# Keys of two attention pairs in one buffer, parted by VectorE: a grouped-query attention kernel on one Trainium2 core

## The chip, the core and the metric

The kernel runs on one NeuronCore of a Trainium2 chip. The core has a matrix engine (TensorE, "PE" in the profile, its weight loads "PEld"), three engines for elementwise work (VectorE "DVE", ScalarE "ACT", GpSimd "POOL"), a queue engine that issues transfers here (SyncE, "SP"), and 16 DMA engines that move data between the chip's memory and the on-chip buffers. The metric is the device time of one execution in microseconds. A profiled execution also has a span, which is the time between its first and its last recorded event.

## What is computed

The reference, cut to what matters:

```
B, Hq, Hkv, Sq, Sk, D = 16, 32, 8, 16, 2048, 128      # all tensors bf16
k = repeat(k, 4, axis=1);  v = repeat(v, 4, axis=1)   # 4 query heads share one key/value head
scores = einsum("bhqd,bhkd->bhqk", q, k) * D ** -0.5
out = einsum("bhqk,bhkd->bhqd", softmax(scores), v)
```

There are 16 * 8 = 128 groups (one key/value head of one batch entry). Each has 4 * 16 = 64 query rows, 512 KB of keys and 512 KB of values. K and V together are 128 MB, read once; queries and output are 2 MB each.

## The kernel before

**Tiling.** Two groups make a pair, so there are NP = 64 pairs, numbered p. Each pair has 1 MB of K, 1 MB of V and 128 rows of queries. Everything is a software pipeline over p, with one loop written out by hand for each engine and semaphores between them. The first four pairs and the last ones are unrolled, the middle runs in a hardware loop of 8 (4 on TensorE).

**One pair, engine by engine.**

- SyncE's queue loads K of a pair into one of 8 buffers `Kn` and V into one of 4 buffers `Vb`. The helper `load` (L178, built on `copy`, L171) describes a 1 MB load as 64 rows of 16 KB on the memory side and 128 partitions of 8 KB on the buffer side, so each row of 16 KB is spread over two neighbouring partitions. Only the first two loads of K are plain (128 rows of 8 KB).
- VectorE's `kt(p)` (L474 to L483, the instruction is L482) turns the keys of a pair: it sees each key's 128 bf16 numbers as 64 f32 words and transposes 32x32 blocks of 2048 words in each partition into one of two buffers `KT`.
- TensorE's `scores(p)` (L353) multiplies the queries `Qs` with `KT` into `S_ps`, the only score buffer in PSUM: it waits for `kt(p)` and for VectorE to have read the scores of the pair before (`sem_max`).
- VectorE's `step(p)` (L490) waits for these scores, reads `S_ps` in two halves, writes them scaled to `Sneg` and takes the row minimum (L502, called max(p) below); then, at odd p, it computes two reciprocals (L488); then it runs `kt(p + 2)`. VectorE runs its instructions in this order and no other.
- GpSimd joins the minima of the two halves (L225 to L233), and ScalarE computes the exponentials (`exp`, L550).
- TensorE transposes the exponentials (`transposes`, L371), ScalarE copies them to `PT` (`evict`, L561), and four pairs later (PVLAG = 4) TensorE multiplies them with V (`product`, L423, or L412 for the last 8 pairs). ScalarE scales the result (`norm`, L574) and stores it: one store of 32 KB a pair for pairs 0 to 39 and for the last one; the outputs of the others are held in `Oh` and stored in six pieces at the end.

**The order of the loads.** SyncE's queue runs one loop over t: K of pair t, then now and then a block of queries, then V of pair t - VLAG with VLAG = 6. A load of K waits until the buffer that it overwrites has been turned (`sem_kt`), a load of V until the product that used its buffer is done (`sem_pv`). The last four V loads go into freed `Kn` buffers and wait for nothing that is late. All these loads are on one queue and land in the order in which they are issued.

**The end.** For the last four pairs TensorE's order is written out by hand (L454 to L470): scores(62), six filler matmuls (`idle`, L433), product(57), scores(63), transposes(61), product(58), product(59), transposes(62), product(60), transposes(63), product(61), five fillers, product(62), three fillers, product(63). ScalarE's order is exp(61), norm(57), exp(62), evict(61), norm(58), exp(63), evict(62), norm(59), evict(63), and then the last norms and the last store. V of pair 63 is loaded in two pieces of 768 KB and 256 KB (L307).

Of the kernel before, what the change touches and what calls it, by code (L numbers as in the profile page):

```python
# [6 lines left out]
ALU = mybir.AluOpType  # L7
# [5 lines left out]
NV = 4  # L13
NKT = 2
NPT = 4
NO = 8
NQ = 2
NR = 8
VLAG = 6
PVLAG = 4  # L20
QLEAD = 3
HELD = (4, 4, 4, 4, 4, 3)
# [3 lines left out]
def bass_standalone__gqa_softmax__sampling_kernel(  # L26
# [3 lines left out]
    v: bass.AP,  # L30
    out: bass.AP,
):

# [19 lines left out]
    sb = lambda name, shape, dt: ctx.enter_context(nc.sbuf_tensor(name, shape, dt))  # L55
    sem = lambda name: ctx.enter_context(nc.semaphore(name))

    iota_t = sb("iota_t", [128, 128], I32)
    ident4 = sb("ident4", [128, 128], F32)
    warm = sb("warm", [128, 2], F32)  # L60
    Kn = [sb(f"Kn{i}", [128, 32 * 128], BF16) for i in range(NK)]
    Vb = [sb(f"Vb{i}", [128, 32 * 128], BF16) for i in range(NV)]
    KT = [sb(f"KT{i}", [128, 32 * 64], F32) for i in range(NKT)]
    Qn = [sb(f"Qn{i}", [128, 4, 128], BF16) for i in range(NQ)]
    Q4 = sb("Q4", [128, 4, 2, 4, 64], BF16)
    QT = [sb(f"QT{i}", [128, 2, 512], F32) for i in range(2)]
# [15 lines left out]
    O_ps = ctx.enter_context(nc.psum_tensor("O_ps", [128, 512], F32))  # L82

    sem_id = sem("sem_id")
    sem_k = [sem(f"sem_k{i}") for i in range(NK)]
    sem_v = [sem(f"sem_v{i}") for i in range(NV)]
    sem_vl = [sem(f"sem_vl{i}") for i in range(2)]
    sem_vx = [sem(f"sem_vx{i}") for i in range(3)]
# [20 lines left out]

    qf = q.rearrange("b h s d -> (b h s) d")  # L110
    of = out.rearrange("b h s d -> (b h s) d")
    kf = k.rearrange("b h s d -> (b h s d)").rearrange("(r x) -> r x", x=4096)
    vf = v.rearrange("b h s d -> (b h s d)").rearrange("(r x) -> r x", x=4096)
    vf4 = v.rearrange("b h s d -> (b h) (s d)").rearrange("g (a x) -> a g x", a=128)

# [15 lines left out]


    def v_tile(p):
        return Kn[p % 4 + (NP - 8) % NK] if p >= NP - 4 else Vb[p % NV]

    def out_tile(p, i):
        return Oh[:, p - PH, :] if isinstance(p, int) and PH <= p < NP - 1 else Osb[i % NO][:, :]
# [48 lines left out]
    with nc.Block() as block:  # L186

        @block.gpsimd
        def _(gp):
            gp.memset(warm[:, :], 0.0).then_inc(sem_id, 1)  # L190
            gp.iota(iota_t[:, :], [[1, 128]], base=0, channel_multiplier=-1).then_inc(sem_id, 1)
            gp.wait_ge(sem_id, 2)
            gp.tensor_scalar(ident4[:, :], iota_t[:, :], 0.0, None, op0=ALU.is_equal).then_inc(sem_id, 1)


            def held(p):
# [79 lines left out]

        @block.sync
        def _(sp):
            def load_k(p):
                s = p % NK  # L280
                if p >= NK:
                    sp.wait_ge(sem_kt, p - NK + 1)
                src = kf[128 * p:128 * (p + 1), :]
                if p < 2:
                    ins = sp.dma_start(Kn[s][:, :], src)
                else:
                    ins = load(sp, Kn[s][:, :], src, 4096, 2)
                ins.then_inc(sem_k[s], 16)

            def load_v(p):  # L290
                if p >= NP - 4:
                    sp.wait_ge(sem_kt, p - 3)
                elif p >= NV:
                    sp.wait_ge(sem_pv, p - NV + 1)
                dst = v_tile(p)[:, :]
                done = sem_vx[p - NP + 4] if NP - 4 <= p < NP - 1 else sem_v[p % NV]
                if p < P4:
                    load(sp, dst, vf[128 * p:128 * (p + 1), :], 4096, 2).then_inc(done, 16)
                    return
                dst = dst.rearrange("a (g x) -> a g x", g=2)  # L300
                src = vf4[:, 2 * p:2 * p + 2, :]
                if p < NP - 1:
                    for h in range(2):
                        load(sp, dst[:, h, :], src[:, h, :], 2048, 2).then_inc(done, 16)
                    return
                for n, x in enumerate((slice(0, 1536), slice(1536, 2048))):
                    sp.dma_start(dst[:, :, x], src[:, :, x]).then_inc(sem_vl[n], 16)  # L307

            def store_held(p, n):
                sp.wait_ge(sem_nm, p + n + 1)  # L310
                src = Oh[:, p - PH:p - PH + n, :]
                copy(
                    sp, of[128 * p:128 * p + 128, :], [[128, 128], [128 * 128, n], [1, 128]],
                    src, [src.ap[0], [1, 1], [1, n * 128]],
                ).then_inc(sem_oh, 16)

            for t in range(NP + VLAG):
                if t < NP:
                    load_k(t)
                for c in range(2, NQC):  # L320
                    if t == 4 * c - QLEAD:
                        if c == NQ:
                            sp.wait_ge(sem_q4d, 2)
                        sp.wait_ge(sem_q4, max(2, 4 * c - 6))
                        load(sp, Qn[c % NQ][:, :, :], qf[512 * c:512 * (c + 1), :], 512, 2).then_inc(sem_q[c % NQ], 16)
                if 0 <= t - VLAG < NP:
                    load_v(t - VLAG)
            p = PH
            for n in HELD:
                store_held(p, n)  # L330
                p += n

        @block.tensor
        def _(pe):
# [3 lines left out]

            def scores(p, i, first=False):
                pe.wait_ge(sem_qs, p + 1)  # L340
                pe.wait_ge(sem_kt, p + 1)
                if not first:
                    pe.wait_ge(sem_max, p)
                kt = KT[i % NKT][:, :].bitcast(BF16).rearrange(
                    "p (w x b l f) -> p w b f x l", w=2, x=16, b=2, l=32)
                qs = Qs[i % 2][:, :, :].rearrange("p b (x f) -> p b f x", f=2)
                for acc in range(4):
                    b, f = divmod(acc, 2)
                    for r in range(4):
                        rows = slice(32 * r, 32 * (r + 1))  # L350
                        h = r // 2
                        for w in range(2):
                            ins = pe.matmul(  # L353
                                S_ps[64 * w:64 * (w + 1), 512 * r:512 * (r + 1)],
                                qs[rows, b, f, 64 * h:64 * (h + 1)],
                                kt[rows, w, b, f],
                                start=(acc == 0), stop=(acc == 3),
                            )
                ins.then_inc(sem_s, 1)
# [29 lines left out]
            def product(p, i, out, tail=False, last=False):  # L389
# [13 lines left out]
                pe.nop(nofuse=True)  # L403
                if isinstance(p, int) and p >= P4:
                    pt = PT[i % NPT][:, :, :].bitcast(BF16).rearrange("p (h t) (w q e) -> p h w t e q", h=2, w=2, e=2)
                    vt = v_tile(p)[:, :].rearrange("p (h j d) -> p h j d", h=2, d=128)
                    for j in range(16):
                        w, t, e = j // 8, j % 8 // 2, j % 2
                        if last and j in (0, 12):
# [5 lines left out]
                            )  # L415
                else:
                    pt = PT[i % NPT][:, :, :].bitcast(BF16).rearrange("p t (w q e) -> p w t e q", w=2, e=2)
                    vt = v_tile(p if isinstance(p, int) else i)[:, :].rearrange("p (x d) -> p x d", d=128)
                    for x in range(32):
                        w, t, e = x // 16, x % 16 // 2, x % 2  # L420
                        for h in range(2):
# [49 lines left out]

        @block.vector
        def _(dve):
            def kt(p, i):  # L474
                src = Kn[i % NK][:, :].bitcast(F32)
                dst = KT[i % NKT][:, :]
                if isinstance(p, int) and p >= P4:

                    src = src.rearrange("p (m x y) -> p m x y", m=2, x=8)
                    dst = dst.rearrange("p (x m y) -> p m x y", m=2, x=8)  # L480
                dve.wait_ge(sem_k[i % NK], 2 * (p - i) + 16 * (i // NK + 1))
                ins = dve.transpose(dst, src)  # L482
                ins.then_inc(sem_kt, 1)  # L483

            def recip(p, i, n):
# [4 lines left out]
            def step(p, i):  # L490
                known = isinstance(p, int)
                dve.wait_ge(sem_s, p + 1)
                if i >= 2:
                    dve.wait_ge(sem_exp, p - 1)
                for h in range(2):
                    if not known or p < P4:
                        dst = Sneg[i % 2][:, :].rearrange("p (t h g l e) -> p h g t l e", t=8, h=2, g=2, e=2)[:, h]
                        src = S_ps[:, 1024 * h:1024 * (h + 1)].rearrange("p (g t e l) -> p g t l e", g=2, t=8, e=2)
                    else:
                        dst = Sneg[i % 2][:, :].rearrange("p (h t g l f) -> p h g t l f", h=2, t=4, g=2, f=4)[:, h]  # L500
                        src = S_ps[:, 1024 * h:1024 * (h + 1)].rearrange("p (g t f l) -> p g t l f", g=2, t=4, f=4)
                    ins = dve.tensor_scalar(  # L502
                        dst, src,
                        -scale, None, op0=ALU.mult, op1=ALU.min, accum_out=own[:, i % NR, h:h + 1],
                    )
                ins.then_inc(sem_max, 1)
                if i >= 3 and i % 2:
                    recip(p - 3, i - 3, 2)
                if not known or p + 2 < NP:
                    kt(p + 2, i + 2)  # L510

            dve.wait_ge(sem_q[0], 16)
            spread(dve, 0, 1).then_inc(sem_q4d, 2)
# [7 lines left out]
        def _(act):  # L521
# [44 lines left out]
            def norm(p, i):  # L566
# [1 line left out]
                act.wait_ge(sem_pv, p + 1)  # L568
                act.wait_ge(sem_rec, p + 1)
                if not isinstance(p, int) or p < PH:  # L570
                    act.wait_ge(sem_o[i % NO], 2 * (p - i) + 16 * (i // NO + 1))
                elif p == NP - 1:
                    act.wait_ge(sem_o[i % NO], 16 * (PH // NO + 1))
                act.activation(  # L574
# [66 lines left out]
```

## Time and profile before

| what | value |
|---|---|
| median of 3 runs | 334.79 us (334.47 to 334.87) |
| the profiled execution: its time, its span | 334.85 us, 333.5 us |
| busy: DVE, PE, ACT, POOL | 294.5, 279.2, 257.7, 149.4 us |
| moved by DMA | 138.61 MB, 416 GB/s over the span |
| one `kt` (L482), 64 of them | 2308 ns |
| one half of max (L502), 128 of them | 1206 ns |
| K load, issue to landing (median) | 20.2 us |
| V load, issue to landing (median) | 18.2 us |

The span and the time of the profiled execution differ by 1.35 us, which lie outside the records. The span is what the views divide into slices and stretches. A "busy" time counts an engine's own instructions, without waits; an engine that is busy most of the time need not be the one that sets the end. "Idle before" an instruction is the time in which its engine had nothing to run, with the event that ended it behind an arrow. Matmul ends are modelled.

### The profile page before, as it was taken

To read this page: it belongs to the slowest core of one execution; us is meant where nothing else is said; L and a number is where in the kernel's file an instruction comes from. 1 tells how busy PE (TensorE), PEld (TensorE's weight loads), DVE (VectorE), ACT (ScalarE), POOL (GpSimd) and SP (SyncE) were. 2 spreads that over 40 slices of the span, in tenths; PEclk is the share of its full clock that TensorE was granted. 3 is DMA by queue.
4 is the path that set the end of the run, shared out by engine and by line. 5 is a ranking of instruction groups with operands and counts; after the bars stand their busy time and mean duration, and the time that the engine had idled before them with its cause. 6 is when DMAs were issued, how large, how long until landed. Compare 5 with 4: busy or idle time off the path is not lost.

```text
span 333.5 us, 16075 instructions
## 1 busy us (share of the span) xinstructions
PE 279.2 (84%) x6542; PEld 209.4 (63%) x6542; DVE 294.5 (88%) x354; ACT 257.7 (77%) x482; POOL 149.4 (45%) x488
## 2 busy tenths in 40 slices
PE   2585988999998999888897988979879798788877
PEld 1253756767676776666665766757757567666465
DVE  3999988999999999989898898998999999989940
ACT  3277877989898989779688787887788687776873
POOL 4444554364544555354445435354363453542320
DMA  8999999999999999999999999999999999999998
GB/s 314 426 419 422 413 419 415 431 424 422 426 423 425 420 428 420 430 418 426 422 427 420 431 419 425 424 423 425 419 421 424 415 423 421 417 425 414 412 405 293
DMA packets 19583, 138.61 MB, mean 416 GB/s; under 512 B 8432, under 2 KB 9712, under 8 KB 10864
## 3 DMA queue, kind: packets, MB, share of 16 engines
q1 hardware_dynamic: 13520, 136.95, 98.1%
q10 hardware_dynamic: 6048, 1.48, 2.0%
q8 instruction: 8, 0.13, 0.2%
q14 instruction: 7, 0.06, 0.0%
HBM read 136.31 MB, written 2.10 MB: 415 GB/s over the span
## 4 chain that ended last, share of the span: by engine, by line
DMA 57%; PE 16%; DVE 15%; issue 8%; ACT 1%; SPq 1%; POOL 1%; DVEq 0%; POOLq 0%; ACTq 0%
DMA Vb<-in_v_dram 43%; PE O_ps L423 9%; DMA Kn<-in_k_dram 8%; DVE KT L482 8%; DVE Sneg L502 7%; DMA Kn<-in_v_dram 5%; PE ST_ps L371 3%; PE S_ps L353 3%; ACT P L550 1%; SPq L173 1%; PE ST_ps L386 1%; POOL nbias L233 0%; PE ST_ps L412 0%; POOL oth L225 0%; POOL oth L228 0%
## 5 line engine op out<-in xcount | busy, mean ns | idle before, releaser
L482 DVE STREAM_TRANSPOSE KT<-Kn 128x2048 f32<-128x2048 f32 x64 | 147.7, 2308 | 20.1 <-DMA Kn<-in_k_dram 19.9
L550 ACT ACTIVATE P<-Sneg,nbias 128x1024 bf16<-128x1024 f32 x128 | 145.9, 1142 | 15.7 <-POOL nbias L233 14.2
L502 DVE TENSOR_SCALAR_CACHE_REDUCE Sneg<-S_ps 128x1024 f32<-128x1024 f32 x128 | 149.9, 1206 | 4.2 <-PE S_ps L353 4.2
L423 PE MATMUL O_ps<-Vb,PT 64*64 64x128 bf16 x3584 | 111.1, 216 | 30.5 <-issue 27.0
L423 PEld LDWEIGHTS O_ps<-Vb,PT 64*64 64x64 bf16 x3584 | 102.8, 107 | 49.3 <-issue 49.3
L561 ACT ACTIVATE PT<-ST_ps 128x512 f32<-128x512 f32 x126 | 68.5, 594 | 16.5 <-PE ST_ps L371 15.9
L353 PE MATMUL S_ps<-KT,Qs 32*64 32x512 bf16 x2048 | 73.5, 396 | 6.0 <-DVE Sneg L502 3.8
L371 PE MATMUL ST_ps<-ident,P 128*128 128x128 f32 x504 | 70.1, 283 | 8.7 <-ACT P L550 8.5
L225 POOL COPY oth<-own 64x4 f32<-64x4 f32 (+1 forms) x65 | 11.9, 183 | 136.4 <-DVE Sneg L502 134.3
L371 PEld LDWEIGHTS ST_ps<-ident,P 128*128 128x128 f32 x504 | 55.1, 143 | 16.9 <-ACT P L550 10.5
L353 PEld LDWEIGHTS S_ps<-KT,Qs 32*64 32x64 bf16 x2048 | 27.3, 106 | 30.4 <-issue 16.6
L207 POOL COPY Qs<-QT 128x512 bf16<-128x512 bf16 x64 | 39.0, 610 | 12.1 <-POOL rowsum L240 5.6
L233 POOL TENSOR_SCALAR nbias<-own,oth 128x1 f32<-128x1 f32 x128 | 33.9, 280 | 10.6 <-POOL oth L228 9.0
L163 POOL COPY Q<-Qn 128x1024 bf16<-128x1024 bf16 x31 | 32.4, 1044 | 1.4 <-DMA Qn<-in_q_dram 1.4
L574 ACT ACTIVATE O<-O_ps,rrec 128x128 bf16<-128x128 f32 x40 | 14.5, 363 | 18.7 <-PE O_ps L423 18.5
L240 POOL TENSOR_TENSOR rowsum<-own,oth 64x1 f32<-64x1 f32 x128 | 23.8, 186 | 8.2
L386 PE MATMUL ST_ps<-ident,Q 128*128 128x128 f32 x128 | 22.5, 304 | 4.6 <-POOL Q L163 4.6
L386 PEld LDWEIGHTS ST_ps<-ident,Q 128*128 128x128 f32 x128 | 14.7, 150 | 18.5 <-issue 18.5
L550 ACT ACTIVATION_READ_ACCUMULATOR P<-Sneg,nbias 128x1 f32 x128 | 24.2, 189 | 0.0
L536 ACT ACTIVATE QT<-ST_ps 128x512 f32<-128x512 f32 x32 | 18.5, 579 | 3.9 <-PE ST_ps L386 3.8
L574 ACT ACTIVATE Oh<-O_ps,rrec 128x128 bf16<-128x128 f32 x20 | 7.3, 367 | 17.3 <-PE O_ps L423 14.4
L228 POOL COPY oth<-own 64x4 f32<-64x4 f32 (+1 forms) x65 | 11.8, 181 | 7.3
(30 smaller groups left out, 44.6 us busy)
## 6 DMA issues: line engine op xcount, KB each, us to landing
Kn<-in_k_dram SPq DMA_DIRECT2D x64, 1024.0 KB, 20.2
Vb<-in_v_dram SPq DMA_DIRECT2D x56, 1024.0 KB, 18.2
Vb<-in_v_dram SPq DMA_DIRECT2D x8, 512.0 KB, 15.4
Kn<-in_v_dram SPq DMA_DIRECT2D x6, 512.0 KB, 14.5
Qn<-in_q_dram SPq DMA_DIRECT2D x15, 128.0 KB, 19.8
out_dram<-O ACTq DMA_DIRECT2D x41, 32.0 KB, 8.9
Kn<-in_v_dram SPq DMA_DIRECT2D x1, 768.0 KB, 17.7
out_dram<-Oh SPq DMA_DIRECT2D x5, 128.0 KB, 11.8
```

Of the source, the lines that this page charges most:

```text
L163: return eng.tensor_copy(Q4[:, :, b, :, :], src.unsqueeze(2).to_broadcast([128, 4, 4, 64]))
L207: gp.tensor_copy(Qs[i % 2][:, :, :], QT[i // 4 % 2][:, :, 128 * x:128 * (x + 1)].bitcast(BF16)).then_inc(sem_qs, 1)
L233: ins = gp.tensor_scalar(nbias[:, s, h:h + 1], own[:, s, h:h + 1], oth[:, s, h:h + 1], None, op0=ALU.min)
L240: gp.tensor_tensor(rowsum[rows, t:t + 1], own[rows, s, 2 + h:3 + h], oth[rows, s, 2 + h:3 + h], op=ALU.add,).then_inc(sem_sum[h], 1)
L353: ins = pe.matmul(S_ps[64 * w:64 * (w + 1), 512 * r:512 * (r + 1)], qs[rows, b, f, 64 * h:64 * (h + 1)], kt[rows, w, b, f], start=(acc == ...
L371: ins = pe.transpose(dst[:, 128 * t:128 * (t + 1)], P[i % 2][:, 128 * x:128 * (x + 1)], ident4[:, :])
L386: ins = pe.transpose(dst[:, 128 * j:128 * (j + 1)], src[:, j, b, :], ident4[:, :])
L423: ins = pe.matmul(out[rows, :], pt[rows, w, t, e, :], vt[rows, x, :], start=(x == 0), stop=(x == 31),)
L482: ins = dve.transpose(dst, src)
L502: ins = dve.tensor_scalar(dst, src, -scale, None, op0=ALU.mult, op1=ALU.min, accum_out=own[:, i % NR, h:h + 1],)
L550: ins = act.activation(to[:, h], of_s[:, h], ACT.Exp, bias=nbias[:, s, h:h + 1], scale=-1.0, accum_out=own[:, t, 2 + h:3 + h],)
L561: act.activation(PT[i % NPT][:, 4 * h:4 * (h + 1), :].rearrange("p t q -> p (t q)"), p_stage_ap(p, h), ACT.Copy,).then_inc(sem_ev[h], 1)
```

## The change

Two pairs now share one K buffer of 16 KB a partition. Of the pair 2n the row i of 16 KB goes to partition 2i, of the pair 2n + 1 to partition 2i + 1. There are four such buffers instead of eight of half the size, so the space is the same. The two KT buffers are twice as large and each holds two pairs; to make room the output ring has four buffers instead of eight and a small table of GpSimd's lies in a KT buffer until that is used.

- A K load is 64 rows of 16 KB to 64 partitions (every other one). The first two pairs come as four loads of 64 rows of 8 KB: first half the columns of both, then the other half.
- `kt(2n)` turns half of the keys of both pairs, `kt(2n + 1)` the other half. The block transpose reads its source in order and writes each second column 16 words further on, so that the two pairs come apart. For the last 8 pairs each `kt` is two instructions of half the size.
- `kt(2n)` waits for both K loads; `kt(2n + 1)` waits for nothing. `scores(p)` of an even p waits for both turns, of an odd p the same count. VectorE runs `kt(2)` and `kt(3)` in step 0, and `kt(p + 3)` instead of `kt(p + 2)` in every later step.
- A load of K waits until both turns of the buffer it overwrites are done. VLAG is 7 instead of 6.
- The access patterns of scores and of max follow the new order of keys.

The core of the diff:

```
-NO = 8
+NO = 4
-VLAG = 6
+VLAG = 7
...
-    Kn = [sb(f"Kn{i}", [128, 32 * 128], BF16) for i in range(NK)]
+    Kn = [sb(f"Kn{i}", [128, 64 * 128], BF16) for i in range(NK // 2)]
-    KT = [sb(f"KT{i}", [128, 32 * 64], F32) for i in range(NKT)]
+    KT = [sb(f"KT{i}", [128, 64 * 64], F32) for i in range(NKT)]
+    iota_t = KT[1][:, 0:128].bitcast(I32)
...
             def load_k(p):
-                s = p % NK
+                n, a = divmod(p, 2)
                 if p >= NK:
-                    sp.wait_ge(sem_kt, p - NK + 1)
-                src = kf[128 * p:128 * (p + 1), :]
-                if p < 2:
-                    ins = sp.dma_start(Kn[s][:, :], src)
-                else:
-                    ins = load(sp, Kn[s][:, :], src, 4096, 2)
-                ins.then_inc(sem_k[s], 16)
+                    sp.wait_ge(sem_kt, 2 * n - NK + 2)
+                dst = Kn[n % (NK // 2)]
+                step = dst[:, :].ap[0][0]
+                for a, y, done in ((a, 0, sem_k[n % (NK // 2)]),) if n else ((0, 4096 * p, sem_kx[p]), (1, 4096 * p, sem_kx[p])):
+                    size = 8192 if n else 4096
+                    r = 64 * (2 * n + a)
+                    copy(
+                        sp, dst[a:a + 1, y:y + size], [[2 * step, 64], [1, 1], [1, size]],
+                        kf[r:r + 64, y:y + size], [[8192, 64], [1, 1], [1, size]],
+                    ).then_inc(done, 16)
...
             def load_v(p):
                 if p >= NP - 4:
-                    sp.wait_ge(sem_kt, p - 3)
+                    sp.wait_ge(sem_kt, p // 2 * 2 - 2)
...
             def scores(p, i, first=False):
                 pe.wait_ge(sem_qs, p + 1)
-                pe.wait_ge(sem_kt, p + 1)
+                pe.wait_ge(sem_kt, p + 2 - i % 2)
...
             def kt(p, i):
-                src = Kn[i % NK][:, :].bitcast(F32)
-                dst = KT[i % NKT][:, :]
-                if isinstance(p, int) and p >= P4:
...
-                dve.wait_ge(sem_k[i % NK], 2 * (p - i) + 16 * (i // NK + 1))
-                ins = dve.transpose(dst, src)
+                n, m = divmod(i, 2)
+                src = Kn[n % (NK // 2)][:, :].bitcast(F32)[:, 2048 * m:2048 * (m + 1)]
+                dst = KT[n % NKT][:, :]
+
+                last = isinstance(p, int) and p >= P4
+                if last:
+                    dst = dst.rearrange("p (x m n z a l) -> p m n x z l a", m=2, n=2, x=8, z=4, a=2)[:, m]
+                    src = src.rearrange("p (n x z l a) -> p n x z l a", n=2, x=8, z=4, a=2)
+                else:
+                    dst = dst.rearrange("p (x m z a l) -> p m x z l a", m=2, x=16, z=4, a=2)[:, m]
+                    src = src.rearrange("p (x z l a) -> p x z l a", x=16, z=4, a=2)
+                if n == 0:
+                    dve.wait_ge(sem_kx[m], 32)
+                elif m == 0:
+                    dve.wait_ge(sem_k[n % (NK // 2)], 4 * (p - i) + 32 * (n // (NK // 2) + (n % (NK // 2) > 0)))
+                for n in range(2 if last else 1):
+                    ins = dve.transpose(dst[:, n], src[:, n]) if last else dve.transpose(dst, src)
                 ins.then_inc(sem_kt, 1)
...
                 if i >= 3 and i % 2:
                     recip(p - 3, i - 3, 2)
-                if not known or p + 2 < NP:
-                    kt(p + 2, i + 2)
+                for n in range(2 if known and p == 0 else 3, 4):
+                    if not known or p + n < NP:
+                        kt(p + n, i + n)
```

## The prediction

> **What bounds the kernel now.** I read the page first, then VectorE's waits, then the chain that ended last, then the last 30 us instruction by instruction.
>
> ```profile
> PE 279.2 (84%) x6542; PEld 209.4 (63%) x6542; DVE 294.5 (88%) x354; ACT 257.7 (77%) x482; POOL 149.4 (45%) x488
> ...
> DMA  8999999999999999999999999999999999999998
> GB/s 314 426 419 422 413 419 415 431 424 422 426 423 425 420 428 420 430 418 426 422 427 420 431 419 425 424 423 425 419 421 424 415 423 421 417 425 414 412 405 293
> ```
>
> The DMA engines are busy from the first slice to the last. The transfers are one continuous stream; the time is a start, that stream, and what is left when the last byte has landed. VectorE, at 88%, is next. Its idle time has one main cause, the landing of K:
>
> ```profile
> DVE KT L482 <- DMA Kn<-in_k_dram: 19.9, 38, 2.7
> ```
>
> (total, times, longest). So each `kt` runs as soon as its K has landed. In the chain that ended last, V transfers hold most of the time behind 111 us, and the last link is V of pair 63. What matters most for this change is how the end is laid out. VectorE's rows:
>
> ```profile
> 313.21 2.31 DVE L482 STREAM_TRANSPOSE KT<-Kn 128x2048 f32<-128x2048 f32 x1 [0.39 <-DMA Kn<-in_k_dram]
> 315.44 1.19 DVE L502 TENSOR_SCALAR_CACHE_REDUCE Sneg<-S_ps 128x1024 f32<-128x1024 f32 x1
> 316.56 0.08 DVE L502 DVE_READ_ACCUMULATOR Sneg<-S_ps 128x1 f32 x1
> 316.56 1.22 DVE L502 TENSOR_SCALAR_CACHE_REDUCE Sneg<-S_ps 128x1024 f32<-128x1024 f32 x1
> 317.70 0.09 DVE L502 DVE_READ_ACCUMULATOR Sneg<-S_ps 128x1 f32 x1
> 319.11 1.22 DVE L502 TENSOR_SCALAR_CACHE_REDUCE Sneg<-S_ps 128x1024 f32<-128x1024 f32 x1 [1.33 <-PE S_ps L353]
> ...
> 321.41 0.08 DVE L502 DVE_READ_ACCUMULATOR Sneg<-S_ps 128x1 f32 x1
> ```
>
> K of pair 63, the last, lands at 313.2; kt(63), max(62), a wait of 1.4 for scores(63), max(63); VectorE is through at 321.4, 8.2 us after the landing. TensorE's rows that follow:
>
> ```profile
> 325.13 1.09 PE L371 MATMUL S_ps<-ident,P 128*128 128x128 f32 x8 [0.56 <-ACT P L550]
> 326.15 1.08 PE L412 MATMUL S_ps<-Kn,PT 128*64 128x128 bf16 x32
> 327.17 1.25 PE L433 MATMUL ST_ps<-ident 128*128 128x512 bf16 x5
> 328.57 1.09 PE L412 MATMUL O_ps<-Kn,PT 128*64 128x128 bf16 x32 [0.15 <-issue]
> 329.59 0.82 PE L433 MATMUL ST_ps<-ident 128*128 128x512 bf16 x3
> 330.46 1.10 PE L412 MATMUL ST_ps<-Kn,PT 128*64 128x128 bf16 x32
> ```
>
> Transposes(63), product(61), fillers, product(62), fillers, product(63): nearly without gaps. V of pair 63 lands at about 330.4 by the chain, and product(63) starts at 330.46. So the compute chain from K of pair 63 and the stream of V end together: **there is no slack in the end.** From product(63) to the end of the span it is 333.5 - 330.46 = 3.05 us. Between the landings of K63 and V63 lie 7 MB of V (pairs 57 to 63): 17.2 us, 2.46 us a MB.
>
> **The change, part by part.**
>
> *The end.* K of pair 63 now has V of pairs 56 to 63 behind it (VLAG 7): 8 MB, 19.7 us before V63 lands, 2.5 us earlier than now. But kt(62) now waits for it too, and kt(62) stands in step 59, kt(63) in step 60. So everything below stands behind that landing on VectorE, in its order: kt(62), max(60), kt(63), max(61), then max(62) and max(63), each behind its scores. A kt: one of 2048 words takes 2.23 us (313.21 to 315.44); now two of 1024 words, taken as two L502 of that length (315.44 to 317.70), 2.3. A max: 2.3. The first four end at 9.2 us. Scores(62): 1.4, as 317.70 to 319.11; max(62) ends at 12.9. Scores(63) stands on TensorE behind scores(62), six fillers and product(57), which now take 4.0 us (312.89 to 316.91); so it starts at 13.2, max(63) at 14.5, and ends at 16.8. From there to product(63) it is 321.41 to 330.46 = 9.05 us, whether V is there or not, as all the links are full; and 3.05 to the end. **The end comes 16.8 + 9.05 + 3.05 = 28.9 us after K63 lands.** By the stream alone it would be 19.7 + 3.05 = 22.75. So the end moves out by **+6.2 us**. This holds however early VectorE is, since kt(62) cannot start before its data. What is late in place of V63 is the chain over VectorE, GpSimd, ScalarE and TensorE. I give it 0.5 us either way (two kt of half size, TensorE's clock with other fillers).
>
> *The stream itself.* The same bytes come in the same order but for one place. A row of 16 KB used to go to two partitions and now goes to one. In the trace's packet records a 16 KB packet takes 625 ns where ScalarE issues no stores (30 to 50 and 250 to 320 us) and 614 ns where it does; the lowest tenth takes 611; the 3 KB packets of the last V load, which go to one partition each, take 125. With u ns a KB and f ns for each partition written, 3u + f = 125 and 16u + 2f = 625 give u = 37.5 and f = 12.5; a 16 KB row to one partition would be 16u + f = 613 (my estimate). A pair's K is 64 packets, 4 an engine. In the 18 or so steps without stores K saves 4 * 12 ns, 0.9 us in all; in the 40 with stores there are 2.7 ns on 8 packets left to gain, 0.9 us at most, and I take 0.6. **-1.5 us.** Ends: 0 (the destination does not count) and all 16 KB packets at 611, (618.5 mean - 611) * 8 an engine and pair * 62 = 3.7 us.
>
> *Steady state.* VectorE turns the same words, 2.3 a pair, and reads the scores in 2.3 + 0.1: 4.6 of the 5.1 us that the stream takes for a pair (20.4 us for 4 pairs in the chain). The wait of kt(2n) for both loads lengthens VectorE's lag by up to one K load, but of two steps it still needs 9.3 of 10.1 us, and behind it only max(p + 1) waits, then scores, transposes and products. V loads are then issued later; they are issued 18.2 us ahead of landing, so 2 to 3 us less leaves the stream unbroken. Cost 0. max reads PSUM in runs of other steps; rows at 301 to 303 us (pattern of the last 8 pairs) and at 16 us take the same 1.22: 0. TensorE reads KT in runs of 16 instead of 32 words; 0, as it has gaps marked "issue" of 27 us.
>
> *The start.* scores(0) now stands behind kt(1) (8.7 to 11.0 us) and takes 2.2 as now; max(0) 13.2 to 15.5; then kt(2) and kt(3) to 20.1, where max(1) starts instead of at 15.4; at 4.6 a step max(4) starts at 33.9 instead of 29.8. So the first V load that waits (V4, issued at 35.9) goes out 4.1 us later, with one more K load (2.5 us) queued ahead of it. The V loads of 20 to 60 us land 8.7 us after issue (median), of which 2.5 are their own and some 2 fixed (a 96 KB store at the end lands in 2.1); 1.6 less leaves 2 us of queue. Cost 0; if TensorE's gaps are longer, up to 0.7. The two extra issues (0.6 us each) and the ring of four output buffers (stores land in 8.9 us, four steps are 20) cost nothing.
>
> **Sum:** 334.85 + 6.2 - 1.5 = 339.55 for a profiled execution; the median stands 0.06 below: **339.5 us.**
>
> **The rivals.**
>
> 1. *The strided write is slow.* VectorE writes each second word 64 bytes further on; no row of before writes so. Nearest rows: L502 reads PSUM with a jump of 128 bytes at every word and takes 1206 ns for 1024 words, L482 in order 2308 for 2048: no word costs more for the jump, which speaks against it. Lower end: 0. Upper end, one word in two cycles: 4.4 us a kt; then VectorE needs 6.8 a step and becomes the bound: 17 + 64 * 6.8 = 452 us. It decides from 2.8 us a kt (slack 0.5 a step). [...] Chance 0.08.
> 2. *64 partitions are loaded at a lower rate.* No load of before goes to 64 partitions. Each 1% on K's half of the stream costs 1.6 us, 5% 8 us: 348. For it: half the partitions take the same bytes; against: every other partition spans the same range, and 16 KB in one piece is what each packet reads anyway. [...] Chance 0.05.
> 3. *Not slower: the cheaper rows pay for the end.* The mechanism is K's packets in the whole stream. It decides at 6.2 us, that is 25 ns on each of 248 K packets an engine, 594 ns for 16 KB. The fastest slice of the page (431 GB/s, 16 engines) comes to 608 ns a packet. At 28 ns a packet the time would be 333.8. Chance 0.09, more than these rows bear out, since the end was laid out from matmul ends that are modelled.
> 4. *Between:* 24 to 25 ns a packet saved, and the end just paid for: 334.8, chance 0.04.
>
> **How the numbers follow.** The forecast has 0.74. Its range: 334.8 + 6.2 - 3.7 - 0.4 = 336.9 to 334.8 + 6.2 + 0.5 + 0.7 = 342.2. The rivals 3 and 4 below (0.13) and the greater part of 1 and 2 above stay out; a mild form of 1 (kt 10% longer: +0.5 at the end) and of 2 (1%) lies inside. A run of this kernel can be told from no change at about 0.2%: faster 0.09, within 0.04, slower 0.87.
>
> **What would show it.** After the change VectorE's last kt rows must read kt(62) released by K at about 309 us, then max, kt, two max with waits for scores; product(63) must start some 26 us after that without waiting for V, and the last slices of the DMA row must be empty (5 to 6 us with nothing to load). kt at 2.3 us speaks against rival 1; GB/s of 420 to 430 in the middle against rival 2. VectorE's waits for K should come at every second kt only, 0.8 us each. If product(63) still starts just as V63 lands, the step on the end is wrong.

## The result and the profile after

| | before | after |
|---|---|---|
| median, us | 334.83 (334.47 to 335.63, 6 runs) | 401.99 (401.34 to 403.18, 6 runs) |
| ratio to before | | 1.2007 (95%: 1.1982 to 1.2031) |
| span of the profiled execution, us | 333.5 | 400.2 |

The changed kernel is a fifth slower: the sign of the forecast is right, its size is not. The shares of the chain that ended last, before:

```profile
DMA 57%; PE 16%; DVE 15%; issue 8%; ACT 1%; SPq 1%; POOL 1%; DVEq 0%; POOLq 0%; ACTq 0%
```

The page of the changed kernel (busy times, the slices, the chain that ended last):

```profile
PE 292.1 (73%) x6542; PEld 218.0 (54%) x6542; DVE 377.6 (94%) x362; ACT 255.7 (64%) x482; POOL 149.4 (37%) x488
...
DMA  8999379999998979999999989989898998985691
GB/s 300 429 426 422 156 269 397 399 401 349 376 397 330 390 303 378 395 367 403 325 393 359 389 329 391 390 324 400 355 382 328 380 380 315 393 314 185 235 368 30
...
DVE 61%; issue 33%; PE 3%; DMA 1%; DVEq 1%; ACT 0%; SPq 0%; POOL 0%; ACTq 0%; POOLq 0%
```

The stream of transfers has holes all the way: behind the first slices 403 GB/s is the best, and the mean over the span is 346. VectorE has 83 us more of busy time than before and now makes most of the chain, 61%; DMA, which held 57% of it, has 1%. The changed kernel's waits of VectorE (total, times, longest):

```profile
DVE Sneg L523 <- PE S_ps L364: 4.7, 3, 2.1
DVE rrec L509 <- POOL rowsum L246: 4.4, 2, 2.9
DVE KT L503 <- DMA Kn<-in_k_dram: 3.6, 1, 3.6
```

Where VectorE waited 38 times for K, it now waits once, for the very first load. It is late, and all others wait for it. Two of its steps, from the changed kernel's timeline (start, length; L503 is the turn, L523 the max, which were L482 and L502):

```profile
151.29 3.77 DVE L503 STREAM_TRANSPOSE KT<-Kn 128x2048 f32<-128x2048 f32 x1
154.88 1.24 DVE L523 TENSOR_SCALAR_CACHE_REDUCE Sneg<-S_ps 128x1024 f32<-128x1024 f32 x1
...
156.00 1.27 DVE L523 TENSOR_SCALAR_CACHE_REDUCE Sneg<-S_ps 128x1024 f32<-128x1024 f32 x1
...
157.22 3.76 DVE L503 STREAM_TRANSPOSE KT<-Kn 128x2048 f32<-128x2048 f32 x1
```

A turn of 2048 words holds VectorE for 3.59 us, start to start (151.29 to 154.88), where it was 2.24; the max takes 2.27 (154.88 to 157.15, where a reciprocal of 0.07 follows), as before. A step is 5.9 us, and the stream needs 5.1. From max(0), which starts at 16.16, to the end of max(63) at 388.45 there is hardly a gap: 64 max of 2.27, 62 turns of 3.6 and 31 reciprocals are 371 of the 372.3 us. The tail behind it takes 11.75 us; it was 12.1 (321.41 to 333.5).

So a single instruction explains the outcome, and it is the one whose write pattern changed. What the rest of the change does is hidden under it. The experiments ask two things: what in the pattern costs the time, and what the change would have done without that.

### The profile page after: what moved, and what is told of

The parts are those of the page before. It is cut to its first block, busy times and chain, and to the rows that moved or that the text cites. A ratio compares the mean times of both kernels' runs of the same rounds, so it can differ in the third digit from the quotient of the medians.

```text
span 400.2 us, 16084 instructions
## 1 busy us (share of the span) xinstructions
PE 292.1 (73%) x6542; PEld 218.0 (54%) x6542; DVE 377.6 (94%) x362; ACT 255.7 (64%) x482; POOL 149.4 (37%) x488
## 4 chain that ended last, share of the span: by engine, by line
DVE 61%; issue 33%; PE 3%; DMA 1%; DVEq 1%; ACT 0%; SPq 0%; POOL 0%; ACTq 0%; POOLq 0%
DVE KT L503 32%; DVE Sneg L523 28%; DMA Kn<-in_k_dram 1%; PE S_ps L364 1%; DVE rrec L509 1%; PE ST_ps L444 0%; ACT P L572 0%; PE S_ps L382 0%; PE ST_ps L423 0%; PE O_ps L423 0%; PE S_ps L423 0%; DVEq L513 0%; DVEq L129 0%; DVEq L501 0%; SPq L179 0%
## 5 line engine op out<-in xcount | busy, mean ns | idle before, releaser
L503 DVE STREAM_TRANSPOSE KT<-Kn 128x2048 f32<-128x2048 f32 (+1 forms) x72 | 239.7, 3349 | 3.6 <-DMA Kn<-in_k_dram 3.6
L523 DVE TENSOR_SCALAR_CACHE_REDUCE Sneg<-S_ps 128x1024 f32<-128x1024 f32 x128 | 152.6, 1244 | 4.7 <-PE S_ps L364 4.7
L364 PE MATMUL S_ps<-KT,Qs 32*64 32x512 bf16 x2048 | 77.9, 413 | 73.9 <-DVE Sneg L523 66.1
L434 PE MATMUL O_ps<-Vb,PT 64*64 64x128 bf16 x3584 | 112.9, 219 | 0.8 <-issue 0.8
L382 PE MATMUL ST_ps<-ident,P 128*128 128x128 f32 x504 | 71.4, 286 | 25.9 <-ACT P L572 25.6
L364 PEld LDWEIGHTS S_ps<-KT,Qs 32*64 32x64 bf16 x2048 | 32.8, 108 | 99.9 <-issue 74.0
L382 PEld LDWEIGHTS ST_ps<-ident,P 128*128 128x128 f32 x504 | 56.2, 145 | 37.4 <-ACT P L572 31.4
L213 POOL COPY Qs<-QT 128x512 bf16<-128x512 bf16 x64 | 38.9, 609 | 12.1 <-POOL rowsum L246 8.5
L397 PE MATMUL ST_ps<-ident,Q 128*128 128x128 f32 x128 | 23.5, 314 | 4.4 <-POOL Q L169 4.4
L523 DVE DVE_READ_ACCUMULATOR Sneg<-S_ps 128x1 f32 x128 | 15.2, 118 | 0.0
```

The lines of the kernel that those rows point to most:

```text
L213: gp.tensor_copy(Qs[i % 2][:, :, :], QT[i // 4 % 2][:, :, 128 * x:128 * (x + 1)].bitcast(BF16)).then_inc(sem_qs, 1)
L364: ins = pe.matmul(S_ps[64 * w:64 * (w + 1), 512 * r:512 * (r + 1)], qs[rows, b, f, 64 * h:64 * (h + 1)], kt[rows, w, b, i % 2, f], start=( ...
L382: ins = pe.transpose(dst[:, 128 * t:128 * (t + 1)], P[i % 2][:, 128 * x:128 * (x + 1)], ident4[:, :])
L397: ins = pe.transpose(dst[:, 128 * j:128 * (j + 1)], src[:, j, b, :], ident4[:, :])
L434: ins = pe.matmul(out[rows, :], pt[rows, w, t, e, :], vt[rows, x, :], start=(x == 0), stop=(x == 31),)
L503: ins = dve.transpose(dst[:, n], src[:, n]) if last else dve.transpose(dst, src)
```

## The experiments

Theory A: VectorE's writes slow down when each word opens another piece of memory than the word before it; a short distance costs nothing. Theory B: an inner loop of two words slows the turn, whatever the distance. Theory C: the turn is slowed by other engines' traffic in the kernel, not by its pattern.

**1. The turn alone.** A small kernel in which VectorE runs 2048 words per partition through one pattern after the other, six times each; a load runs ahead of it and one store of zeros beside its first instructions, and nothing else. The lines of its core (each is a line number below):

```
L48  transpose(B in order,                     A in order)
L49, L50, L51, L52, L53, L54, L55
     transpose(B "p (y a l) -> p y l a",       A "p (y l a) -> p y l a")   a=2, l=2,4,8,16,32,64,1024
L58  the same with a=16, l=2;   L59  a=64, l=32
L60, L61  "p (y a l r) -> p y l a r"           a=2; l=8, r=2;  l=4, r=4     (runs of r words)
L62  transpose(B in order,                     A "p (y a l) -> p y l a")   a=2, l=16
L63, L64, L65  tensor_scalar: in order; written as in L52; read as in L62
```

> This kernel computes nothing of the reference: it loads 1 MB of K, turns it on VectorE alone with one destination pattern after another (2048 words a partition, each pattern 6 times, nothing beside it), and stores zeros. Three theories of the slow turn (3.75 us in the changed kernel, 2.31 before). A, lines: a word that opens another piece of memory than the word before it costs more, and a short distance costs nothing. Then: in order 2.3 us; pairs of columns parted by 2 words 2.3; by 16 words and more 3.7; runs of 4 words parted by 16 words 2.3 to 2.5; whole rows at a step of 8 words as slow as alternation. B, the inner loop: a pattern whose innermost count is 2 costs more whatever the distance. Then 3.7 at every distance with a count of 2, and 2.3 to 2.5 with a count of 64 at a step of 32 words. C, not the write: other engines or the transfers into the same partitions slow the turn. Then every form takes 2.3 here.

Groups of its lines by shape (count, busy time, mean ns of one):

```profile
L50 DVE STREAM_TRANSPOSE B<-A 128x2048 f32<-128x2048 f32 x6 | 22.8, 3805 | 0.2
L54 DVE STREAM_TRANSPOSE B<-A 128x2048 f32<-128x2048 f32 x6 | 22.4, 3730 | 0.2
L59 DVE STREAM_TRANSPOSE B<-A 128x2048 f32<-128x2048 f32 x6 | 21.8, 3636 | 0.2
L64 DVE TENSOR_SCALAR_CACHE_REDUCE B<-A 128x2048 f32<-128x2048 f32 x6 | 21.7, 3616 | 0.2
L52 DVE STREAM_TRANSPOSE B<-A 128x2048 f32<-128x2048 f32 x6 | 21.6, 3599 | 0.2
L62 DVE STREAM_TRANSPOSE B<-A 128x2048 f32<-128x2048 f32 x6 | 14.1, 2354 | 0.2
L65 DVE TENSOR_SCALAR_CACHE_REDUCE B<-A 128x2048 f32<-128x2048 f32 x6 | 14.0, 2328 | 0.2
L58 DVE STREAM_TRANSPOSE B<-A 128x2048 f32<-128x2048 f32 x6 | 13.9, 2312 | 0.2
L60 DVE STREAM_TRANSPOSE B<-A 128x2048 f32<-128x2048 f32 x6 | 13.9, 2312 | 0.2
L49 DVE STREAM_TRANSPOSE B<-A 128x2048 f32<-128x2048 f32 x6 | 13.9, 2311 | 0.2
L63 DVE TENSOR_SCALAR_CACHE_REDUCE B<-A 128x2048 f32<-128x2048 f32 x6 | 13.7, 2286 | 0.2
```

The rows fall into two classes with nothing between. When each word is written 12 bytes or more from the word before, a turn costs 3.60 to 3.81 us: L50 (16 bytes ahead and 12 back by turns), L52 (64 and 60, the change's), L54 (256 and 252). With at most 8 bytes from word to word (L49; L58 but for one word in 32), or in runs of two words with the next run 64 bytes on (L60), it costs 2.31, the same as in order. The length of the inner loop does not decide: L49 has two words and takes 2311 ns, L59 has 64 and takes 3636. The scaling does the same as the transpose (L64 against L63, 3616 against 2286). And the same jump on the read side costs next to nothing (L62 2354 against 2311 in order, L65 2328 against 2286). B falls, C falls (almost nothing ran beside it), and A holds for writes in what it says of the distance: 8 bytes cost nothing (L49), 12 and 16 cost 1.5 us (L50). What the "piece" is, the runs do not show. The price is 0.63 to 0.73 ns a word. The change's pattern takes 3.60 alone and 3.76 in the kernel (56 turns of this shape); the cause of that 0.16 stays open.

**2. The write pattern alone, in the kernel before.** Everything as before, but each turn but the last eight parts its columns as if two pairs were mixed.

```diff
+                else:
+                    src = src.rearrange("p (y l a) -> p y l a", l=16, a=2)
+                    dst = dst.rearrange("p (y a l) -> p y l a", l=16, a=2)
```

> The kernel before with one part of the change alone: the turns of pairs 0 to 55 write each second word 16 words further on (the keys then stand in another order than V, so the attention is mixed up; the last 8 pairs are turned as before). Theories A and B: a turn takes 3.7 us, VectorE needs 5.85 us a pair and sets the pace: 11 + 56 * 5.85 + 8 * 5 + 10 = 389 us, 380 to 397. Theory C: 334 to 336 us.

386.73 us, ratio 1.1552 (1.1531 to 1.1573): the write pattern alone, without the change's buffers, loads and waits, costs 52 us. Its turn, by shape:

```profile
L485 DVE STREAM_TRANSPOSE KT<-Kn 128x2048 f32<-128x2048 f32 x64 | 227.3, 3553 | 2.8 <-DMA Kn<-in_k_dram 2.8
```

The mean takes in the eight turns left in order; with these at 2.31, the other 56 average 3.73. The change as a whole stands 15.3 us higher; its turns take 12.4 us more together (239.7 us, L503), mainly because its last eight pairs are scattered too. The remaining 2.9 us are not accounted for.

**3 and 4. The change with the turn in order.** TensorE then picks out every second word instead. VLAG is 7 (inorder_v7) and 10 (inorder_v10).

```diff
-                    dst = dst.rearrange("p (x m z a l) -> p m x z a l", m=2, x=16, z=4, a=2)[:, m]
+                    dst = dst.rearrange("p (x m y) -> p m x y", m=2, x=16)[:, m]
...
-                    "p (w x b a l f) -> p w b a f x l", w=2, x=32, b=2, a=2, l=16)
+                    "p (w x b l a f) -> p w b a f x l", w=2, x=32, b=2, a=2, l=16)
```

> The changed kernel with the turn writing in order; TensorE picks every second word of KT instead (the same sums, in the same key order). All else as in the change: rows of 16 KB, pairs of K in one buffer, the order of the loads. Theories A and B: a turn takes 2.3 us, the transfers bound it again, and what is left of my prediction is tested: the end comes 28.9 us after the last K lands, 339.5 us (337 to 342), with TensorE's last product waiting for no V; if the end is not bound that way, 333 to 334. Theory C: still about 400 us. If TensorE reads every second word slowly, its 32 score matmuls take more than 1.1 us a pair; twice as long would still lie under the 5.1 us of the stream.

> As the kernel with the turn in order, and V lags K by 10 pairs instead of 7 (VLAG 10), so that the last K has 11 MB of V behind it, 27.1 us, instead of 8 MB, 19.7 us. If the chain behind the last K sets the end (28.9 us), this moves K forward by 7.4 us and the end comes 4.9 to 6 us earlier than with 7: about 333.5 to 334.5 us, and the last product waits for V again. If the end is bound by V already, the two kernels take the same. A start that starves the transfers (V arrives too late for the first product at about 34 us) would add some us to both views.

352.93 us (ratio 1.0547, 1.0532 to 1.0563) and 352.06 (1.0502, 1.0481 to 1.0523). The turn is back at 2.3, and 49 us are gone, but the rest was misjudged. The score matmuls before, and the page of inorder_v7:

```profile
L353 PE MATMUL S_ps<-KT,Qs 32*64 32x512 bf16 x2048 | 73.5, 396 | 6.0 <-DVE Sneg L502 3.8
```

```profile
PE 328.1 (93%) x6542; PEld 214.4 (61%) x6542; DVE 297.6 (85%) x362; ACT 259.8 (74%) x482; POOL 150.2 (43%) x488
...
L364 PE MATMUL S_ps<-KT,Qs 32*64 32x512 bf16 x2048 | 126.3, 607 | 11.0 <-DVE KT L503 5.7
```

TensorE takes one of a pair of bf16 numbers at each step, and neighbours now lie 8 bytes apart instead of 4. One score matmul takes 607 ns instead of 396 (413 in the changed kernel), the 32 of a pair 1.95 us instead of 1.1. That makes TensorE the bound at 93%, and VectorE waits 34.6 us for scores. These two runs therefore say nothing about the end of the kernel, which was their purpose; VLAG makes no difference where TensorE sets the pace.

**5. The change with a turn that writes runs of two words.** KT holds the one half of the columns and then the other, 8 KB further on, and the turn moves two neighbouring words at a time. With the loads as they are, the two pairs come out mixed; every transfer, instruction and wait is that of the change.

```diff
-                    dst = dst.rearrange("p (x m z a l) -> p m x z l a", m=2, x=16, z=4, a=2)[:, m]
-                    src = src.rearrange("p (x z l a) -> p x z l a", x=16, z=4, a=2)
+                    dst = dst.rearrange("p (a x m z e) -> p m x z a e", a=2, x=16, m=2, e=2)[:, m]
+                    src = src.rearrange("p (x z a e) -> p x z a e", x=16, a=2, e=2)
...
-                    "p (w x b a l f) -> p w b a f x l", w=2, x=32, b=2, a=2, l=16)
+                    "p (a w x b l f) -> p w b a f x l", a=2, w=2, x=32, b=2, l=16)
```

> The changed kernel with the turn writing runs of two words (columns 0 and 1 to one pair, 2 and 3 to the other, and so on; KT holds the one pair's half ahead of the other's). The loads are those of the change, so a pair's keys are mixed with its neighbour's: the scores belong to no pair, all instructions and bytes are the same. Theory: two words on a line make the turn cost 2.3 us again, TensorE reads KT in order as in the change, the transfers bound the kernel, and the rest of my prediction is what is left: the end 28.9 us behind the landing of the last K, 339.5 us (337 to 342), the last product waiting for no V. Rival: the chain behind the last K sets nothing, the end comes 3.05 us behind the last V: 333 to 334. Second rival: TensorE or the half of KT further off cost something again: over 343.

341.72 us (339.95 to 342.9), ratio 1.0200 (1.0162 to 1.0238); the profiled execution 340.99, its span 339.7. With the turn at 2.31 this is the kernel that the prediction described. VectorE's waits and GB/s by slice:

```profile
DVE KT L503 <- DMA Kn<-in_k_dram: 23.1, 22, 3.7
```

```profile
GB/s 276 430 438 418 424 392 408 363 415 426 431 424 426 422 431 428 427 425 429 422 420 435 427 424 426 425 428 423 427 424 421 428 419 425 426 424 410 410 383 63
```

The stream is whole again, but for a dip in the sixth to eighth slice, 42 to 68 us. VectorE's timeline at the end, and TensorE's:

```profile
311.29 2.37 DVE L503 STREAM_TRANSPOSE KT<-Kn 128x1024 f32<-128x1024 f32 x2 [1.05 <-DMA Kn<-in_k_dram]
313.58 1.18 DVE L523 TENSOR_SCALAR_CACHE_REDUCE Sneg<-S_ps 128x1024 f32<-128x1024 f32 x1
...
315.84 2.37 DVE L503 STREAM_TRANSPOSE KT<-Kn 128x1024 f32<-128x1024 f32 x2
318.13 1.19 DVE L523 TENSOR_SCALAR_CACHE_REDUCE Sneg<-S_ps 128x1024 f32<-128x1024 f32 x1
...
321.85 1.23 DVE L523 TENSOR_SCALAR_CACHE_REDUCE Sneg<-S_ps 128x1024 f32<-128x1024 f32 x1 [1.30 <-PE S_ps L364]
...
325.60 1.23 DVE L523 TENSOR_SCALAR_CACHE_REDUCE Sneg<-S_ps 128x1024 f32<-128x1024 f32 x1 [1.37 <-PE S_ps L364]
```

```profile
335.86 0.82 PE L444 MATMUL ST_ps<-ident 128*128 128x512 bf16 x3
336.61 1.09 PE L423 MATMUL ST_ps<-Kn,PT 128*64 128x128 bf16 x32
```

K of pair 63 releases kt(62) at 311.29; then come kt, max, kt, max, and two max behind waits for scores; product(63) follows 25.3 us after the landing, without waiting for V, and the end 3.1 later: 28.4 us.

**6. More V behind the last K.** The kernel of 5 with VLAG 6, 8 and 10 (one line each).

> The kernel with runs of two words (the pairs of each buffer mixed as there), V 6 pairs behind K, the value of the kernel before. Theory: the end stands 28.4 us behind the landing of the last K (311.3 to 339.7 with 7). That K now has 7 MB of V behind it instead of 8, so it lands 2.46 us later and the end with it: 344 us. The start has one K load less queued ahead of the V load that waits, so it may lose 1 to 2 us more: up to 346. Rival (the end is bound by V or by something else): no change against 7.

> As before, with 8. K lands 2.46 us earlier against V, and one more K load is queued at the start, where 7 ran dry (408 and 363 GB/s in two slices). By the chain behind the last K alone: 341.7 - 2.5 - 1 to 2 = 337 to 338. Where V is what the products wait for (as with 10, whose turns wait for no K), the pipeline follows V, which lands one K load later than with 7: 340 to 341.

> The same with V 10 pairs behind K instead of 7, the pairs mixed as well. If the chain behind the last K sets the end, K lands 7.4 us earlier against V, the end goes back to the last V and the time to 333 to 334 us, that is the time before less what the cheaper rows of K save (1.5 us, 0 to 3.7). If the end was bound by V already: as with 7. If the start runs out of work (V lands too late for the first products): later than with 7.

| VLAG | median, us | ratio (95%) | K63 landed, us | product(63) behind it | start of the stream, us |
|---|---|---|---|---|---|
| 6 | 345.53 | 1.0333 (1.0307 to 1.0359) | 319.00 | 25.3 | 97.8 |
| 7 | 341.72 | 1.0200 (1.0162 to 1.0238) | 311.29 | 25.3 | 93.0 |
| 8 | 337.40 | 1.0078 (1.0064 to 1.0092) | 307.83 | 25.6 | 90.9 |
| 10 | 340.66 | 1.0164 (1.0134 to 1.0194) | earlier; kt(62) starts at 311.20 | 25.3 (behind kt(62)) | 90.8 |

The landings and the last two columns are from the profiled executions (that of VLAG 6 took 348.72 us, 3.2 above its median, so that its row stands too high). The last column is the time in which the loading queue moved its bytes from 2 to 40 MB, by the trace's packet records; the kernel before has 91.6. From 6 to 8 the chain behind K63 stays the same and only its start moves: each step of VLAG puts 1 MB (2.46 us) more behind K63, and it fills the stream's gap at the start. From 7 to 8 that is 2.5 + 2.1 = 4.6 us; the medians differ by 4.3, the landings of the two profiled executions by 3.5. From 6 to 7 the rows give 2.5 + 4.8, the medians 3.8. At 10 the expected gain did not come. The waits of VectorE there, and the longest of TensorE:

```profile
DVE Sneg L523 <- PE S_ps L364: 24.7, 44, 2.8
DVE rrec L509 <- POOL rowsum L246: 4.4, 2, 2.9
DVE KT L503 <- DMA Kn<-in_k_dram: 4.1, 1, 4.1
```

```profile
PE O_ps L434 <- issue: 25.2, 31, 1.8
```

No turn waits for K any more after the first; max waits for scores instead. The wait ahead of the products, marked "issue", is one for V: from 113 to 305 us each product that TensorE had to wait for (38 of them) starts 0.09 to 0.14 us after a V load has landed, where with VLAG 7 none waits after 58 us. TensorE's scores stand behind these products, and the pipeline follows V. With 8 the turns still wait for K (19 times) and the products for V. The GB/s row of VLAG 8, the best of these, shows no dip at the start:

```profile
GB/s 256 433 434 419 423 417 418 426 424 425 426 422 430 426 422 427 427 428 422 421 423 435 419 425 431 421 427 429 417 429 421 430 421 424 423 430 408 408 399 132
```

**7. The same, computed in full.** K of a pair as two loads of 512 KB to every fourth partition, so that two neighbouring words belong to one pair.

```diff
-                    copy(
-                        sp, dst[a:a + 1, y:y + size], [[2 * step, 64], [1, 1], [1, size]],
-                        kf[r:r + 64, y:y + size], [[8192, 64], [1, 1], [1, size]],
-                    ).then_inc(done, 16)
+                    for e in range(2):
+                        copy(
+                            sp, dst[2 * a + e:2 * a + e + 1, y:y + size], [[4 * step, 32], [1, 1], [1, size]],
+                            kf[r + e:r + 64, y:y + size], [[2 * 8192, 32], [1, 1], [1, size]],
+                        ).then_inc(done, 16)
```

> The same turn with loads that fit it: a pair's rows go to partitions 4j + 2a and 4j + 2a + 1, as two transfers of 512 KB (32 partitions each, rows of 16 KB, every second row of memory) in place of one of 1 MB. All that the reference computes is computed. If 32 partitions a transfer load as fast as 64: as the mixed kernel with 7, 339.5 by my theory. If transfers to 32 partitions are slower, each 1% on K costs 1.6 us, and the GB/s of the middle slices fall below 420.

> The same with V 10 pairs behind K. All of the reference is computed. If both theories hold (two words on a line, end set by the chain behind the last K): 333 to 334 us, a little faster than before. If the transfers of 32 partitions are slower, 335 and more.

342.96 us (ratio 1.0240, 1.0206 to 1.0273) and 342.17 (1.0210, 1.0180 to 1.0240): 1.2 and 1.5 us over the mixed ones, with 426 and 425 GB/s from 110 to 230 us (before 424). The 333 to 334 us expected with VLAG 10 did not come here either. With this write pattern the change costs 2%, not 20%. VLAG 8, the best of the mixed ones, was not run in this form.

**8. The end without its late fillers.** The eight filler matmuls ahead of product(62) and product(63) are taken out, in the kernel of 5 and in the kernel before.

```diff
-IDLE = (6, 5, 3)
+IDLE = (6, 0, 0)
```

> As the kernel with runs of two words and 7 (pairs mixed), without the five and three filler matmuls ahead of the last two products. If TensorE's chain sets the end, the end moves forward by what they took, 1.25 + 0.82 = 2.1 us: 339.6. If V set the end: no change, 341.7.

> The control: the kernel before without the same eight fillers. By my reading its end is set by the last V (product(63) starts 0.05 us after it): no change, 334.5 to 334.9; up to 0.5 us later if TensorE's clock falls without them.

340.60 us (ratio 1.0173, 1.0156 to 1.0189) and 335.24 (1.0023, 0.9998 to 1.0047). In the kernel of 5 product(63) stands 23.2 instead of 25.3 us behind the landing of K63:

```profile
313.07 2.37 DVE L503 STREAM_TRANSPOSE KT<-Kn 128x1024 f32<-128x1024 f32 x2 [0.60 <-DMA Kn<-in_k_dram]
336.24 1.06 PE L423 MATMUL ST_ps<-Kn,PT 128*64 128x128 bf16 x32
```

In this profiled execution K63 landed 1.8 later, so that less of it shows in the time: the median falls by 1.1 us where 2.1 were expected, and the intervals of the two ratios overlap, so the gain rests on the trace more than on the time. In the kernel before nothing is won that a measurement can tell. TensorE's timeline there:

```profile
328.33 1.20 PE L412 MATMUL O_ps<-Kn,PT 128*64 128x128 bf16 x32 [1.44 <-issue]
330.11 1.10 PE L412 MATMUL ST_ps<-Kn,PT 128*64 128x128 bf16 x32 [0.58 <-DMA Kn<-in_v_dram]
```

Both products now wait, the last one for V, and it starts at 330.11 where it started at 330.46. So the end of the kernel before is set by the stream, and that of the kernel of 5 by the chain of work: the same edit shortens the chain by 2.1 us in the one and only opens waits in the other.

## Why the prediction was wrong

**Steady state: the step that failed.** It put a kt at 2.3 us and the jump at nothing, and gave the opposite, rival 1, a chance of 0.08. The turn holds VectorE for 3.6, the step 5.9 us; the threshold that the rival named, 2.8 us a kt, is passed by far, and the price is 402.0 - 341.7 = 60.3 us of the 67.2. The rival had the place, the cause (the strided write) and the point of decision right; its ends of 2.3 and 4.4 us a kt held the value. No run shows the 4.4: it was the author's estimate, about twice the 2.23 of a kt before, and the slowest pattern of experiment 1 took 3.81. The fixed part of 17 us in the rival's sum was too small: 16.2 us to the first max and the tail of 11.75, less the two turns (7.2) that the 64 steps count as well, are 20.8. That the kernel is slower was forecast for another reason, the end; in this kernel the turn hides it, so the right sign says nothing for the mechanism, and the end has to be read in experiment 5. There VectorE waits for K 22 times, 1.05 us each, where every second kt and 0.8 were forecast.

What led astray was the choice of the nearest row. L502 reads PSUM in jumps of 128 bytes at no cost that its row shows (1206 ns for 1024 words, where L482 takes 2308 for 2048); it was set against a *write* to SBUF in jumps of 64. Reading and writing are not the same: a scattered read of SBUF costs 2354 ns, a scattered write 3599, the same words in order 2311 (experiment 1). A row shows a price only for its own direction and memory, and no row of before had a write of this kind. With ends of 2.3 and 4.4 us, and three quarters of the way between them above the threshold, a chance of 0.08 was too small.

**TensorE's runs of 16 at no cost: right.** The 32 score matmuls of a pair take 1.15 to 1.18 us at the end of experiment 5, 1.12 before, and max waits no longer for them (1.30 and 1.37 us; 1.33 before). In experiment 3 the same thought (it has room) failed, since a step of 8 bytes is another thing than a shorter run (607 ns a matmul against 413).

**The end: right.** It can be read in experiment 5. 28.4 us from K63's landing, put at 28.9; the links in the order given (the fourth ends at 9.1, max(63) at 16.6, product(63) starts at 25.3; put at 9.2, 16.8 and 25.85); product(63) without a wait for V. Against the 22.75 of the stream alone it makes +5.7, put at +6.2. K63 itself landed at 311.3, put at about 309; that is the start, below.

**The stream itself: right.** Packets of 16 KB average 620 ns from 250 to 300 us, where no stores run (625 before; put at 613 for K and 625 for V, so 619), and 612 from 110 to 230 us, where they do (615 before). In the first stretch 37% of them now take under 616 ns, with a median of 612, and the others 624; before it was 1%. That is a saving of 12 ns on some packets and none on the rest, as was estimated for K and V. Its bytes from 40 to 120 MB took 190.2 us, before 191.3; over all of them that makes 1.7 us, put at 1.5.

**The start: under-sized.** V4 went out at 41.59 instead of 35.87, 5.7 us later, put at 4.1; 0.9 of it is kt(0), which starts at 7.14 instead of 6.21. The queue ran dry at 42 to 68 us, and about 2.2 us were lost (the shortfall of the three slices of 392, 408 and 363 GB/s against 425), put at 0 with 0.7 as the end of the range. VLAG 8 restores it (experiment 6).

The sum with these sizes: 333.5 + 5.7 - 1.7 + 2.2 = 339.7, the span of experiment 5. Its median of 341.72 lies inside the forecast's range and 2.2 above the forecast; 0.7 of that is the distance of the median from the profiled execution, which stays open. **Rival 2 is out:** loads to 64 partitions kept the stream at 426 GB/s (110 to 230 us, before 424), loads to 32 at 425 to 426. **Rivals 3 and 4 are out:** a K packet saved about 12 ns, where 24 to 25 were needed. (Rival 3's 333.8 us is a slip: its sum, 334.8 + 6.2 - 28 ns * 248, gives 334.1.)

## What to carry to other kernels

Before a rearrangement is moved into an instruction's access pattern, look at its write side first: VectorE here writes as fast as in order when two neighbouring 4-byte words come one after the other (2.31 us for 2048 words), and at about five eighths of that rate when each goes 12 bytes or more away (3.60 to 3.81), so keep the runs at 8 bytes, or gather on VectorE's read side (2.35). TensorE's read side is no such refuge: its step of 8 bytes cost 607 ns against 396. A price taken from a row is shown for that row's engine, direction and memory alone; where no row has the same three, the case that would overturn the forecast deserves a real chance, in proportion to how much of its bounds lies beyond the point of decision. And an engine with half a microsecond of room per step in a stream is a bound in waiting: work out from what price it decides before anything else.

## What the runs showed of the hardware that was not expected

- VectorE, 2048 f32 words a partition: 2.29 to 2.31 us when written in order, at steps of up to 8 bytes or in runs of two or four words; 3.60 to 3.81 when each word goes 12 bytes or more from the last, for the block transpose and for a scaling alike; scattered reads 2.33 to 2.35.
- TensorE reading bf16 at a step of 8 bytes instead of 4: 607 instead of 396 ns for a matmul of 32x512.
- Loads to every second or every fourth partition lose nothing (426 and 425 to 426 GB/s from 110 to 230 us, before 424). With K's rows of 16 KB going to one partition instead of two, 37% of the 16 KB packets take 612 ns instead of 624.
- A row's mean can rise without the engine being slower: max has 1244 ns after against 1206 before, and takes the same 2.27 us for both halves start to start.
